# Attention and two MoE layers on one core: scratch in a later weight's place, eight early loads, and unread products on TensorE

## The chip, the cores and the metric

The kernel runs on one core of one Trainium2 chip. The metric is the device time of one execution in microseconds (us). TensorE is PE in the profile (its weight loads are PEld), VectorE is DVE, ScalarE is ACT, GpSimd is POOL, SyncE is SP. DMAs are asked for on SP, on ACT or on POOL; in the kernel before only SP and, late in the program, POOL ask for any. TensorE's clock has two levels, 1.2 and 2.4 GHz.

## The reference

Three layers, float32 (the weights of the first MoE come as 8-byte floats):

```python
# attention: q, k, v of (4, 8, 576, 64), s of (4, 8, 576)
cum = cumsum(maximum(s, 0), -1)
bias = -(cum[..., :, None] - cum[..., None, :])
scores = where(causal, -1e9, q @ k.T / sqrt(64) + minimum(bias, 0))
x = softmax(scores) @ v                      # reshaped to (2304, 512)
# first MoE layer: a dense gated block, 512 -> 2048 -> 512
h = x @ w_in
x = (h * sigmoid(1.702 * h)) @ w_out
# second MoE layer: 8 experts, every token in each of them, 512 -> 1024 -> 512
P = exp(logits - max); eight rounds of row and column normalisation, times N / E
out = sum over e of P[:, e] * (relu(x @ w1[e]) @ w2[e])
```

The running sums of `s` go into the scores as extra rows of the q and k operands.

## The kernel before, in words

The program is a list of instructions for each engine, and the order of each list is fixed when the kernel is built. A planner in the file (class `Sequencer`) sets it: it gives each instruction a cost and an earliest time, keeps a planned clock for each engine, and issues an engine's instructions in the order of their planned times. A loop near the end of the file (`while moe1_can is not None`) picks TensorE's next piece of work: the first of six kinds (scale of v, transposed x, values, transposed scores, scores, first MoE) that the plan holds ready. Where nothing is ready it moves TensorE's planned clock on, by at most 100 planned ns at a time, and looks again. So a wrong cost changes the order of the instructions, and nothing else.

Attention goes in groups of 8 heads: tokens 0 to 255 of a batch (one unit of work for each head), then tokens 256 to 575 (three units). A unit has scores (tile `sp`, on PE), a masked maximum (`sm`, `stats`, on DVE), an exponential (on ACT), a transpose (`tp`, on PE), a copy (`pf`, on ACT or DVE), the values (`op`, on PE), and a division into `xg` (DVE). The first eight heads take q and k as they come, in float32, from the tile `kf`: 64 rows by one DMA, and 2 rows of running sums by a second, from the small tile `aux0`, which DVE has to compute first (`sums(0, 256)`). There are four `kf` buffers (`N_KF`), so that heads 4 to 7 are loaded when earlier heads are done with theirs. Later heads load `kq`, split it into a rounded part and a rest (`one`, `two`) and fetch their rows of sums from DRAM (`aux_d`, written by `sums_left`, which the program comes to after the third unit of scores).

When 256 tokens are done they are transposed (`xtp`, `xh`, `xl`), and the first MoE can run on them: `mm1` makes 24 products into `hp`, and `mm2` 24 into `acc` (`accx`, `accw`), for each of 8 pairs of weight tiles. The weights come as chunks `st`, four to a pair, and ACT and DVE turn each into a rounded part and a rest (`wih`, `wil`, `woh`, `wol`). The memory holds four pairs (`NP0`) while the scratch of the early attention is allocated. The running sums (`aux0`, `aux`, `cum`) have a pool of their own, `auxpool`; when it is done, heads 8 to 15 take its place through `spool2`. The second MoE follows after the first and takes two thirds of the time; the change does not touch it.

Every DMA of the hardware queues reports on one of eight semaphores, in turn over all of them and whichever engine asks for it, and a DMA waits, on the engine that asks, until the last one on the same semaphore has landed. In the rows of the built program they stand as DMAHW0 to DMAHW7.

Of the kernel before, what the change touches and what calls it, by code (L numbers as in the profile page):

```python
# [38 lines left out]
N_KF = 4  # L39
# [18 lines left out]
class Sequencer:  # L58
# [96 lines left out]
    def submit(self, engine, what, call, outs, ins, adds=False):  # L155
        op = Op()
# [4 lines left out]
        if what == "dma_start":  # L161
            op.cost = 60 if engine == "SP" else 1000
            op.nbytes = self.size(outs[0]) * outs[0].shape[0] * (2 if self.fine and outs[0].dtype == F16 else 4)
            if adds and self.fine:
                op.nbytes *= ADDING
        else:
            sums = len(outs) > 1
            if engine == "PE":
                op.load = 110 if BYTES[ins[0].dtype] == 4 else 27
            op.cost = self.cost(engine, what, outs[0], ins, sums)  # L170
            op.tail = {"DVE": 85, "ACT": 110}.get(engine, 0) + 90 * sums
# [31 lines left out]
    def issue(self, op):  # L203
# [9 lines left out]
        if op.nbytes:  # L213
            self.issued = max(self.issued, start) + 475
            self.dma = max(self.dma, self.issued + 1200) + op.nbytes / 360
            op.end = self.dma + 440 + op.late
# [119 lines left out]
def kernel(  # L336
# [42 lines left out]
    NP0, NP1 = 4, 7  # L379
# [13 lines left out]
    alloc_w(wpool, range(NP0))  # L393
# [11 lines left out]
    su_aux = ExitStack()  # L405
    auxpool = Pool(seq, su_aux.enter_context(tc.tile_pool(name="auxpool", bufs=1, side=left, reuse_waits="tile")))
    aux0 = auxpool.tile([BH, 4, 256], F32, name="aux0")
    aux = auxpool.tile([2 * BH, 4, S], F32, name="aux")
    cum = auxpool.tile([2 * BH, 2, S], F32, name="cum")
# [37 lines left out]
    def sums_left():  # L447
# [4 lines left out]
        for t, p, r, by in ((1, slice(BH, 2 * BH), 0, 8.0), (0, slice(0, BH), 2, -1.0)):  # L452
# [6 lines left out]
            nc.sync.dma_start(out=aux_d[:, :, t], in_=aux[p])  # L459

# [115 lines left out]
    spool2 = []  # L576

    def place_of(n):
        if n < H:
            return spool  # L580
        if n >= 2 * H:
            return apool
        if not spool2:
            su_aux.close()
            spool2.append(Pool(seq, su.enter_context(
                tc.tile_pool(name="spool2", bufs=1, side=left, reuse_waits="tile")
            ), aux.tensor.name))
        return spool2[0]

# [12 lines left out]
    def load_qk(n):  # L602
# [3 lines left out]
        if n < H:  # L606
            kq = spool.tile([66, kend + nq], F32, tag="kq", name="kf", bufs=N_KF)
            nc.sync.dma_start(out=split_qk(kq[0:64], q0), in_=of_qk(qk[b, h, 0:64], n))
            nc.sync.dma_start(out=kq[64:66], in_=aux0[b * H + h:b * H + h + 1])
            qk_of[n] = (kq,)  # L610
            return
        kq = place_of(n).tile([128, kend + nq], F32, tag="kq", name="kq", bufs=3 if n < 2 * H else 1)
# [20 lines left out]
    def load_more():  # L633
        nonlocal n_qk
        while n_qk < min(len(heads), n_scored + 1 + N_KF if n_qk < H else n_prep + (3 if n_qk < 2 * H else 1)):
            if n_qk == H and (n_s < 3 or auxpool.held()):
                return
# [311 lines left out]
    def do_score():  # L949
# [13 lines left out]
        if n_s == 3:  # L963
            sums_left()
# [185 lines left out]
    def convert():  # L1150
# [12 lines left out]
        if c == 4 * NP0 and stage[0] is spool:  # L1163
            if n_s < NU and units[n_s][0] < 2 * H - 2 or n_v < NU and units[n_v][0] < 2 * H - 2:
                return
            if min(n_pv, n_prep) < 2 * H or spool.held() or spool2[0].held():
                return
# [8 lines left out]
        if c == 4 * NP1 and NP1 not in wih:  # L1176
# [5 lines left out]
            )), range(NP1, NPAIR))  # L1182
        seq.rank = 2
# [669 lines left out]
    seq.holding = True  # L1853
    sums(0, 256)
    for n_qk in range(1, 3):
        load_qk(n_qk - 1)
# [53 lines left out]
    def first_moe():  # L1910
# [3 lines left out]
        def can(j):  # L1914
            p = at_pair[j]
            if p == NPAIR or 4 * p + 2 > n_conv:
# [3 lines left out]
                seq.settled(wih[p].tensor.name), seq.settled(wil[p].tensor.name),  # L1920
            )

        def second(i):
            def when():
# [3 lines left out]
                t = max(seq.settled(x.tensor.name) for x in (gh, gl, woh[p], wol[p]))  # L1928
# [9 lines left out]
        for item in range((NB1 - 2) * NPAIR):  # L1938
# [6 lines left out]
            if (j, p) == (1, 0):  # L1945
                lent[0] = True
            mm1(j, p, 0)
# [62 lines left out]
    while moe1_can is not None:  # L2010
# [14 lines left out]
        if which is None:  # L2025
            stuck += 1
            assert stuck < 3000
            seq.free["PE"] = min(min(times), now + 100)
# [252 lines left out]
```

## Time and profile before

| | us |
|---|---|
| median of 3 runs (2004.87 to 2005.23) | 2005.07 |
| the profiled execution, whole | 2004.55 |
| its span, from the first instruction to the last | 2002.8 |
| PE busy in the span (15683 products) | 1963.7 |
| DVE busy | 1472.6 |
| ACT busy | 1252.9 |

The profiled execution is 0.5 us below the median, and 1.75 us of it lie outside its span. The rows come from one execution: start and length of instructions, what they waited for, the busy time of each engine in a stretch, and PEclk, the granted TensorE clock as a share of 2.4 GHz. The ends of matmuls are modelled, so the distance from one start to the next says more of the speed of TensorE than the length does.

### The profile page before, as it was taken

Reading aid. Unit: us, or ns where it says so; the run is one execution under the profiler, and the core shown is the slowest. Engines: PE = TensorE matmul, PEld = TensorE weight load, DVE = VectorE, ACT = ScalarE, POOL = GpSimd, SP = SyncE. Lnnn points to the kernel's source line nnn. Section 1 sums busy time; section 2 is a strip of 40 time slices with the busy share of each in tenths; the row PEclk is TensorE's granted clock in tenths of the full one; section 3 lists DMA queues with packets and bytes.
Section 4 is the critical chain, followed back from the end, with each engine's and each line's share of the span. In section 5 each row is a group of like instructions: output and inputs, shape, how many; then the busy total and the mean of one; then the engine's idle time right before and its main releaser. Section 6 shows DMA issues by size and latency. Waiting matters only on the chain.

```text
span 2002.8 us, 40907 instructions
## 1 busy us (share of the span) xinstructions
PE 1963.7 (98%) x15683; PEld 1581.9 (79%) x15683; DVE 1472.6 (74%) x3416; ACT 1252.9 (63%) x2581; POOL 87.5 (4%) x144
## 2 busy tenths in 40 slices
PE   7999999999999999999999999999999999999999
PEld 6889999999988677777777777777777777777777
DVE  5887799887753676988877766776786876777656
ACT  5887677666644575666666666656666666665333
POOL 0000000000000000000000111111101001111000
PEclk9989999999999999999999999999999999999999
DMA  7455345444226454475475566767557556666331
GB/s 222 157 187 172 115 141 171 133 119 123 75 69 213 156 197 151 158 257 182 156 256 144 132 183 176 182 170 204 161 129 245 151 150 185 165 171 182 119 129 43
DMA packets 230100, 322.11 MB, mean 161 GB/s; under 512 B 38272, under 2 KB 156224, under 8 KB 229904
## 3 DMA queue, kind: packets, MB, share of 16 engines
q1 hardware_dynamic: 216944, 295.90, 45.2%
q0 software_dynamic: 12960, 23.60, 8.3%
q8 instruction: 123, 2.02, 0.4%
q14 instruction: 73, 0.60, 0.1%
HBM read 230.85 MB, written 84.34 MB: 157 GB/s over the span
## 4 chain that ended last, share of the span: by engine, by line
PE 81%; DVE 9%; ACT 6%; DMA 3%; issue 1%; SPq 0%; POOL 0%; ACTq 0%; DVEq 0%; POOLq 0%
PE C L294 16%; PE A L294 16%; PE D L294 16%; PE hp L294 8%; PE B L294 8%; PE acc L294 5%; PE sp L294 3%; PE op L294 3%; PE tp L294 2%; ACT h L294 2%; PE accw L294 2%; DVE h L294 2%; DVE hst L294 1%; DMA kq<-in_qk_dram 1%; PE accx L294 1%
## 5 line engine op out<-in xcount | busy, mean ns | idle before, releaser
L294 PEld LDWEIGHTS <-h 128*128 128x128 f16 x6048 | 591.4, 98 | 85.6 <-issue 6.9
L294 PEld LDWEIGHTS <-w1o 128*128 128x128 f16 x4036 | 394.6, 98 | 255.1 <-issue 4.4
L294 PE MATMUL C<-xt,w1o 128*128 128x384 f16 x1152 | 218.6, 326 | 1.4 <-DVE hst L294 1.4
L294 PE MATMUL D<-xt,w1o 128*128 128x384 f16 x1152 | 218.4, 326 | 0.0
L294 PE MATMUL D<-w2o,h 128*128 128x256 f16 x1728 | 217.7, 273 | 0.2 <-ACT y L294 0.2
L294 PE MATMUL A<-xt,w1o 128*128 128x384 f16 x1152 | 214.8, 326 | 0.1
L294 PE MATMUL A<-w2o,h 128*128 128x256 f16 x1728 | 212.2, 273 | 1.8 <-ACT B L294 1.6
L294 PE MATMUL C<-w2o,h 128*128 128x256 f16 x1728 | 208.4, 273 | 1.8 <-DVE y L294 1.7
L294 DVE SCALAR_TENSOR_TENSOR h<-hst,h 128x768 f16<-128x768 f32 (+1 forms) x192 | 138.7, 751 | 56.0 <-ACT h L294 56.0
L294 ACT COPY C<-B 128x384 f32<-128x384 f32 (+1 forms) x168 | 71.5, 426 | 153.6 <-PE B L294 92.6
L294 PE MATMUL hp<-xh,wih 128*128 128x256 f32 (+1 forms) x512 | 156.3, 305 | 0.5 <-DVE t L294 0.5
L294 PE MATMUL hp<-xl,wih 128*128 128x256 f32 (+1 forms) x512 | 154.0, 301 | 0.0
L294 PE MATMUL hp<-xh,wil 128*128 128x256 f32 (+1 forms) x512 | 153.3, 299 | 0.0
L294 POOL DMA_DIRECT2D acc_d<-y x90 | 78.0, 867 | 1219.6 <-DVE y L294 660.3
L294 ACT ACTIVATE h<-hst 128x768 f16<-128x768 f32 (+1 forms) x192 | 126.2, 678 | 3.8 <-DVE hst L294 3.7
L294 ACT ACTIVATE sm<-sm,stats 64x576 f32<-64x576 f32 (+4 forms) x160 | 93.0, 601 | 41.6 <-DVE stats L294 41.2
L294 PE MATMUL acc<-gh,woh 128*128 128x256 f32 x384 | 111.1, 289 | 0.0
L294 PE MATMUL B<-w2o,h 128*128 128x256 f16 x864 | 110.5, 273 | 0.1
L294 PE MATMUL B<-xt,w1o 128*128 128x384 f16 x576 | 109.3, 326 | 0.0
L294 PE MATMUL acc<-gl,woh 128*128 128x256 f32 x384 | 108.5, 282 | 0.0
L294 PE MATMUL acc<-gh,wol 128*128 128x256 f32 x384 | 108.3, 282 | 0.0
L294 ACT COPY B<-A 128x384 f32<-128x384 f32 (+1 forms) x168 | 70.3, 426 | 57.9 <-PE A L294 57.2
(235 smaller groups left out, 3880.3 us busy)
## 6 DMA issues: line engine op xcount, KB each, us to landing
xt<-xc_d SPq DMA_DIRECT2D x168, 384.0 KB
wm<-in_moe_w_dram SPq DMA_DIRECT2D x112, 256.0 KB
w2o<-w_d SPq DMA_DIRECT2D x56, 512.0 KB
wr<-in_moe_w_dram SPq DMA_DIRECT2D x112, 256.0 KB
w_d<-wo SPq DMA_DIRECT2D x98, 256.0 KB
acc_d<-y POOLq DMA_DIRECT2D x90, 256.0 KB, 5.0
kq<-in_qk_dram SPq DMA_DIRECT2D x32, 448.0 KB
st<-in_moe_w_in_dram SPq DMA_DIRECT2D x16, 512.0 KB
```

The lines of the kernel that those rows point to most:

```text
L294: self.seq.submit(self.name, what, lambda: method(*args, **named), outs, ins, "accum_op" in named)
```

## The change

- The running sums get no pool of their own. They lie in `auxw`, a tile in the place where the fifth pair of weights goes later, so `NP0` is 5. `sums_left` is called at the start, right behind `sums(0, 256)`.
- `kf` of the first eight heads lies in two buffers each of the first MoE's tiles `gh`, `gl`, `t` and two of its own. All eight are asked for at the start; six of the eight loads, and the rows of sums of every second head, are asked for on ACT. Heads 8 to 15 have two `kq` buffers (three before).
- TensorE gets products of a constant bf16 tile `filler` into `unread`, which nothing reads: 14 of 512 columns at the start, and one of 128 columns at every second look of the loop that finds nothing ready for over 100 planned ns, until the first MoE's first piece.
- The planner holds TensorE at its high level from the end of the 14 on, counts a DMA on SP as 450 planned ns in place of 60 up to the second MoE, one on ACT as 600, and looks at parts of tiles where it looked at whole ones.

```diff
-N_KF = 4
+N_FILL = 14
-            op.cost = 60 if engine == "SP" else 1000
+            op.cost = 1000 if engine == "POOL" else 600 if engine == "ACT" else 60 if self.fine else 450
-            self.issued = max(self.issued, start) + 475
+            self.issued = max(self.issued, start) + 475 if self.fine else start + op.cost
-    NP0, NP1 = 4, 7
+    NP0, NP1 = 5, 7
-    alloc_w(wpool, range(NP0))
+    alloc_w(wpool, range(NP0 - 1))
+    auxw = wpool.tile([128, 32 * 128], F32, tag="last", name="auxw")
-    aux0 = auxpool.tile([BH, 4, 256], F32, name="aux0")
-    aux = auxpool.tile([2 * BH, 4, S], F32, name="aux")
-    cum = auxpool.tile([2 * BH, 2, S], F32, name="cum")
+    aux0 = auxw[2 * BH:3 * BH, 0:1024].rearrange("p (r s) -> p r s", r=4)
+    aux = auxw[0:2 * BH, 0:4 * S].rearrange("p (r s) -> p r s", r=4)
+    cum = auxw[0:2 * BH, 4 * S:6 * S].rearrange("p (t s) -> p t s", t=2)
+    filler = spool.tile([128, 512], BF16, name="filler")
+    nc.vector.memset(filler, 1.0)
+    unread = ps_m.tile([128, 512], F32, tag="acc0", name="unread")
+    def fill(n):
+        nc.tensor.matmul(unread[:, 0:n], lhsT=filler[:, 0:128], rhs=filler[:, 0:n], start=True, stop=True)
-            kq = spool.tile([66, kend + nq], F32, tag="kq", name="kf", bufs=N_KF)
-            nc.sync.dma_start(out=split_qk(kq[0:64], q0), in_=of_qk(qk[b, h, 0:64], n))
-            nc.sync.dma_start(out=kq[64:66], in_=aux0[b * H + h:b * H + h + 1])
+            tag = ("gh", "gl", "t", "kf")[n // 2]
+            kq = (spool if tag == "kf" else mpool).tile([128, kend + nq], F32, tag=tag, name="kf", bufs=2)[0:66]
+            ask = nc.scalar if n > 1 else nc.sync
+            ask.dma_start(out=split_qk(kq[0:64], q0), in_=of_qk(qk[b, h, 0:64], n))
+            ask = nc.scalar if n % 2 else nc.sync
+            ask.dma_start(out=kq[64:66], in_=aux0[b * H + h:b * H + h + 1])
-        kq = place_of(n).tile([128, kend + nq], F32, tag="kq", name="kq", bufs=3 if n < 2 * H else 1)
+        if n < 2 * H:
+            kq = spool.tile([128, kend + nq], F32, tag="kq", name="kq", bufs=2)
+        else:
+            kq = apool.tile([128, kend + nq], F32, tag="kq", name="kq", bufs=1)
-        if n_s == 3:
-            sums_left()
+    for _ in range(N_FILL):
+        fill(512)
+    seq.cold = False
     sums(0, 256)
+    sums_left()
...
-            seq.free["PE"] = min(min(times), now + 100)
+            if filling[0] and stuck % 2 and min(times) > now + 100:
+                fill(128)
+            else:
+                seq.free["PE"] = min(min(times), now + 100)
```

The list of ACT at the program's start, before, with buffer numbers (the rows `sm` are the exponentials of the units, `pf` is a copy):

```order
L294 ACT_TABLE_LOAD
L294 COPY stats_124<-stats_124 128x1
L294 ACTIVATE sm_231<-sm_231,stats_124 128x128
L294 ACTIVATE sm_231<-sm_231,stats_124 128x256
L294 ACTIVATE sm_244<-sm_244,stats_124 128x128
L294 ACTIVATE sm_244<-sm_244,stats_124 128x256
L294 ACTIVATE sm_265<-sm_265,stats_124 128x128
L294 COPY pf_280<-tp_276 128x384
```

and the same place now (`kf_221` to `kf_228` are heads 0 to 7) and with the semaphores that each row waits for:

```order
L294 COPY stats_119<-stats_119 128x1 [waits Pool_49]
L294 DMA kf_223<-in_qk_dram 64x2x256 [waits DMAHW1_49]
L294 DMA kf_224<-in_qk_dram 64x2x256 [waits DMAHW3_49]
L294 DMA kf_225<-in_qk_dram 64x2x256 [waits DMAHW4_49]
L294 DMA kf_226<-in_qk_dram 64x2x256 [waits DMAHW5_49]
L294 DMA kf_227<-in_qk_dram 64x2x256 [waits DMAHW6_49]
L294 DMA kf_228<-in_qk_dram 64x2x256 [waits DMAHW7_49]
L294 DMA kf_222<-auxw_88 2x1x512 [waits DMAHW1_49,DVE_49]
L294 DMA kf_224<-auxw_88 2x1x512 [waits DMAHW2_49]
L294 DMA kf_226<-auxw_88 2x1x512 [waits DMAHW3_49]
L294 DMA kf_228<-auxw_88 2x1x512 [waits DMAHW4_49]
L294 ACTIVATE sm_268<-sm_268,stats_119 128x128 [waits DVE_49]
```

Ten DMAs have come to stand ahead of ACT's first exponential, the rows of sums of head 1 behind the loads of heads 2 to 7.

The list of SP at the start, now (the rows from the third DMA on; `vf` are values, `aux_d` the sums in DRAM):

```order
L294 DMA vf_131<-in_v_dram 128x8x64
L294 DMA vf_132<-in_v_dram 128x8x64
L294 DMA kf<-auxw 2x1x512 [waits DVE_49,Pool_49]
L294 DMA kf<-auxw 2x1x512 x2
L294 DMA kf<-auxw 2x1x512 [waits DMAHW0_49]
L294 DMA aux_d<-auxw 128x1x576 [waits DMAHW2_49,DVE_49,Pool_49]
L294 DMA aux_d<-auxw 128x1x576 [waits DMAHW0_49,DVE_49]
L294 DMA st<-in_moe_w_in_dram 128x2x512 [waits DMAHW5_49]
```

SP asks for the sums of heads 0, 2, 4 and 6, on semaphores 5, 6, 7 and 0; before, it asked for those of heads 0 to 3 here, and for `aux_d` only after those of heads 4 to 7.

The list of PE at the end of the 14 long products, as a piece of the difference (`unread` is the new product, `sp` with `kf` the scores of the first heads, two rows to a head):

```order
+L294 MATMUL unread<-filler 128x512
+L294 LDWEIGHTS filler
+L294 MATMUL unread<-filler 128x128
+L294 LDWEIGHTS filler
+L294 MATMUL unread<-filler 128x128
 L294 MATMUL sp<-kf 128x128
 L294 MATMUL sp<-kf 128x256
 L294 MATMUL sp<-kf 128x128
 L294 MATMUL sp<-kf 128x256
+L294 LDWEIGHTS filler
+L294 MATMUL unread<-filler 128x128
```

Before, the list begins with the scores of heads 0, 1 and 2 and the first transposes. Now two short products stand ahead of the scores of heads 0 and 1, and two behind them; then, as before, come the scores of head 2 and the first transposes. Up to the first `hp` there are 59 short products: 4 at these two places, 15 in runs of 8 and 7 before the last values of the first eight heads, and 40 in runs of 5, 3, 2, 16 and 14 between those values and the transposes of heads 8 and 9. The run of 16 stands right behind the eight `xtp`, and the run of 14 behind the `vbp` that follows it. The first `hp` now come in two runs of 12 with scores, values and transposes around them; before, the first was one run of 24.

## Rows read from the trace of the kernel before

**Rows 1.** Windows: stretch, length, busy time (instructions) of each engine, PEclk, DMA share, GB/s
```profile
12.64:35.80 23.16, 22.44 (x93) 20.03 (x91) 13.98 (x56) 15.01 (x32) 0.14 (x1) 1.00 0.88 264
35.80:43.92 8.12, 4.51 (x15) 3.54 (x16) 7.97 (x24) 5.21 (x9) 0.00 (x0) 1.00 0.54 152
43.92:48.00 4.08, 4.08 (x19) 3.74 (x18) 3.99 (x10) 2.95 (x5) 0.00 (x0) 1.00 0.66 228
...
48.00:100.00 52.00, 47.89 (x386) 41.87 (x384) 43.41 (x134) 44.30 (x79) 0.88 (x6) 0.99 0.52 162
...
120.00:180.00 60.00, 55.29 (x473) 53.42 (x471) 52.94 (x138) 50.61 (x104) 0.29 (x2) 0.89 0.61 190
180.00:582.00 402.00, 397.25 (x3874) 379.70 (x3873) 323.10 (x972) 267.14 (x552) 3.20 (x22) 1.00 0.45 128
```

**Rows 2.** Timeline of PE, 46 to 49 us: start, length, instruction, [idle before <-releaser]
```profile
45.92 0.41 PE L294 MATMUL hp<-xh,wil 128*128 128x256 f32 x1
46.14 0.41 PE L294 MATMUL hp<-xh,wih 128*128 128x256 f32 x1
...
48.16 0.28 PE L294 MATMUL hp<-xl,wih 128*128 128x256 f32 x1
48.28 0.28 PE L294 MATMUL hp<-xh,wil 128*128 128x256 f32 x1
```

**Rows 3.** Timeline of PE, 99 to 170 us: the waits ahead of low stretches
```profile
99.66 0.60 PE L294 MATMUL vbp<-vd,ones_b 8*128 8x16 f32 x2 [2.03 <-DVE vd L294]
...
118.41 0.36 PE L294 MATMUL sp<-two 68*128 68x256 f32 x1 [2.46 <-DMA two<-one]
...
123.28 0.88 PE L294 MATMUL tp<-ident,sm 128*128 128x128 f32 x3 [2.25 <-DVE stats L294]
...
169.93 0.45 PE L294 MATMUL sp<-one 128*128 128x384 f32 x1 [1.66 <-DVE stats L294]
```

**Rows 4.** Windows over the three stretches in which the granted clock is low
```profile
99.20:106.02 6.82, 6.36 (x46) 6.06 (x47) 5.99 (x18) 2.44 (x5) 0.17 (x1) 0.50 0.15 42
119.69:126.51 6.82, 4.57 (x30) 4.38 (x28) 6.09 (x22) 5.54 (x15) 0.00 (x0) 0.50 0.26 71
170.88:177.71 6.83, 6.35 (x37) 5.80 (x38) 4.96 (x11) 5.05 (x10) 0.14 (x1) 0.50 0.35 106
```

**Rows 5.** Timeline of DVE, 10 to 18 us: first maximum, and the second half's sums
```profile
10.45 0.29 DVE L294 CUSTOM_DVE_ANT_0 sm<-sp,mask 128x128 f32<-128x128 f32 x1 [4.86 <-PE sp L294]
...
12.16 0.31 DVE L294 TENSOR_SCALAR cum<-cum 64x320 f32<-64x320 f32 x1
...
16.20 1.53 DVE L294 SCALAR_TENSOR_TENSOR aux<-cum,aux 32x576 fp32r<-32x576 f32 x2
```

**Rows 6.** Timeline of SP's queue (SPq), 1 to 21 us
```profile
1.50 1.25 SPq L294 DMA_DIRECT2D kf<-in_qk_dram  x2
...
5.73 2.62 SPq L294 DMA_DIRECT2D kf<-aux  x4
...
20.44 0.89 SPq L294 DMA_DIRECT2D st<-in_moe_w_out_dram  x1
```

**Rows 7.** Chain of waits, first 50 us: start, length, what
```profile
5.73 2.80 DMA kf<-aux
```

**Rows 8.** Timeline of ACT, 10 to 23 us
```profile
10.78 0.85 ACT L294 ACTIVATE sm<-sm,stats 128x128 f32<-128x128 f32 x2 [7.66 <-DVE stats L294]
...
22.42 0.67 ACT L294 ACTIVATE st<-st 128x512 f32<-128x512 f32 x1 [1.03 <-DMA st<-in_moe_w_out_dram]
```

**Rows 9.** Timeline of PE, 12 to 15 us
```profile
12.64 0.85 PE L294 MATMUL tp<-ident,sm 128*128 128x128 f32 x3
13.28 1.49 PE L294 MATMUL sp<-kf 66*128 66x128 f32 x4
14.56 0.85 PE L294 MATMUL tp<-ident,sm 128*128 128x128 f32 x3
```

**Rows 10.** Page, costliest groups: count, busy us, mean ns of one, idle before
```profile
L294 PEld LDWEIGHTS <-h 128*128 128x128 f16 x6048 | 591.4, 98 | 85.6 <-issue 6.9
```

## What I predicted before the run

> **What bounds the kernel now.** I read three views in this order. First the busy time by stretches, to see where TensorE (PE) is not full. From 180 to 582 us it is busy for 397.25 of 402 us [rows 1], and nothing that the change does can win more than the 4.75 us there. Before 180 us it is not: of the 60 us from 120 on it misses 4.7, of the 52 us from 48 on 4.1, of the 8.12 us from 35.80 on 3.6 [rows 1]. In these stretches VectorE (DVE) is busy for 52.94 of 60, 43.41 of 52 and 7.97 of 8.12 us: where PE waits there, DVE is mostly what it waits for.
>
> Second, PE's timeline, for its speed. At 46 us two neighbouring products of 256 columns start 0.22 us apart, at 48.2 us 0.12 apart [rows 2]. 256 columns in 0.213 us is 1.2 GHz. So PE runs at its low level until about 48 us, although PEclk reads 1.00 there. The scores of the first heads say the same from the start: one head has 128 and 256 columns in four float32 passes, 1536 columns, and its four records take the 1.28 us from 13.28 to 14.56, which is again 1.2 GHz [rows 9]. From 12.64 to 35.80 us PE is busy for 22.44 of 23.16 us, with DVE at 13.98 and ScalarE (ACT) at 15.01 [rows 1]. So the first eight heads are bound by a slow PE, and 23 us of busy PE did not lift the level: it rose in the first run of 24 dense `hp`. At the high level those 22.44 us would be 11.2.
>
> Here the Trainium skill bears on the reading: "TensorE: Matmul & The Clock Gate", section "Seeing it yourself", says that the recorded clock events were seen to be unreliable on trn2 and should be checked against the durations. By the record alone (1.00), the low start would not exist, and holding the level would be worth nothing; this trace has 0.22 against 0.12 us, so the durations decide.
>
> Third, the waits. PE falls to 0.50 at 99.20, 119.69 and 170.88 us and stays there for 6.82 us each time [rows 4]; ahead of each fall it had idled for 2.03, 2.46 and 1.66 us in one piece, the last with further short waits behind it, and a wait of 2.25 us lies inside the second low stretch [rows 3]. That is the measure for the new idle time below: a gap of some 2 us is enough to lose the level.
>
> **The change part by part.** The sum is made against the profiled execution (2004.55, span 2002.8) and put on the median of 2005.07, which is 0.5 higher.
>
> *Start of the scores.* The 14 long products need only a constant, so they can start as soon as DVE has written it, some 1.4 us into the span by the engines' first rows (SP's first loads stand at 1.5 [rows 6]). At the low level 512 columns are 0.427 us (twice 0.213), 14 of them 6.0 us, and they end near 7.4. They are as dense as the `hp` that lifted the level, so I expect the high level by their end. Now what follows them. The sums of head 0 are asked for on SP 0.31 us later than before, since the second half's maximum stands ahead of the scan on DVE [rows 5]: 5.73 + 0.31 = 6.04, and they land 2.80 us later [rows 7], at 8.84. Head 0's scores then take 0.64 us at the high level and end at 9.48. Head 1's sums stand on ACT, behind the loads of heads 5, 6 and 7, and these wait on the semaphores 5, 6 and 7 that SP's sums of heads 0, 2 and 4 hold. At 0.65 us for an issue (four of SP's took 2.62 [rows 6]): head 5's load goes at 8.84, head 6's at 9.49, head 7's at 10.14, head 1's sums at 10.79, and they land 2.80 later, at 13.59. PE idles from 9.48 to 13.59, 4.1 us. The other end: issues on ACT that cost nothing, and landings after 1.98 us (a 512 KB chunk went from its issue at 20.44 to its reader at 22.42 [rows 6, 8]): 6.04 + 1.30 + 1.98 = 9.32, and 11.30 for head 1; the gap is then 11.30 less (8.02 + 0.64), 2.6 us. Both ends are over 2.03 us, so the level is lost again before head 1, and the first eight heads run at 1.2 GHz as they did.
>
> Then the first transposes wait for head 1 (1.28), two short products (0.2) and head 2 (1.28): 13.59 + 2.76 = 16.35, against 12.64 before [rows 9]; at the other end 14.06. That is +3.7 or +1.4; I take +3.0, nearer to the end whose durations are of the same DMA. Queued behind ACT's ten DMAs is the first exponential: 10.79 + 4 x 0.65 = 13.4 in place of 10.78 [rows 8]. The transposes wait for it, but PE is at head 2 until 16.35, so it costs nothing more. SP's next rows, `aux_d`, wait for DVE's sums; weight chunks stand behind them and are not needed for 30 us.
>
> The skill weighs this otherwise: "DMA: Bandwidth & Descriptors", section "Issuing engines are not separate DMA queues", says that a second issuing engine only saves the sequencer's time to initiate a DMA, which is usually small beside the DMA. By that alone the start would cost 0.31 and no more, and the sum below would be 2.7 lower (2007.4). No row of before shows a DMA on ACT; what it waits for is read from the new list of instructions.
>
> *Short products.* 55 of the 59 lie between head 1's scores and the first `hp`. At the low level 128 columns take 0.107 us, half of 0.213; with a load of 128 columns (98 ns in the page [rows 10]) that nothing hides, 0.2. That is 5.9 or 11 us. At the other end they are free, where PE would have waited: before, it idled for 0.72 us up to 35.80 and for 3.61 up to 43.92 [rows 1]. But 8 score rows of the next heads now stand in the same place (about 2.5 us at the low level), and the plan counted PE twice as fast as it will run, so that PE gets to most of these products late. I take 5.9 less 1.4 hidden, +4.5 (ends 0 and +11).
>
> *When the level rises.* Before, at 48 us, inside the first 24 `hp`. Now the runs of 16 and 14 may lift it a little earlier, or the broken `hp` (12 and 12) may not lift it until the next run of 24. The PE work from the second run of short products to the first `hp` is some 5 us, from there to the run of 24 about 8 at the high level: -4 to +8. I take 0.
>
> *The other sums.* The second half's sums (six rows from the one of 0.31 us to the pair of 1.53, 3.7 us together [rows 5]) move from between the scores into the 4.86 us in which DVE idles ahead of its first maximum [rows 5]. Between the scores PE was the bound, so the gain is nothing (0 to -3.7). Without that cover, head 0's first maximum would start at their end, and PE is waiting for head 1 in any case.
>
> *Fifth pair, two `kq` buffers, dearer SP in the plan.* They reorder everything after the first `hp`. At stake is what is lost between 80 and 182 us: the waits of rows 3 and half of the busy time at the low level, (6.36 + 4.57 + 6.35) / 2 = 8.6 us [rows 4]. The wait of 2.46 us for `two<-one` is one that a plan with dear SP issues should see coming: -2.5. A buffer less could add another like it (+2.5), and the ends for the whole reorder are -17 (all waits of rows 3, 8.4, and the 8.6) and +10 (two more falls of 3.2 us each with their gaps of 2).
>
> Sum: +3.0 + 4.5 + 0 - 2.5 = +5.0, so 2010.1 us.
>
> **The rivals.**
> 1. *The level holds through the first eight heads; faster.* Place: head 1's scores. It decides at a gap of about 2 us: if her sums land within that of head 0's end, PE never idles as long as it did ahead of the three falls. Price: 22.44 us of PE become 11.2, but DVE has 13.98 us to do there, and at the share it reaches later (43.41 of 52, 0.83 [rows 1]) that is 16.8, so the 23.16 us shrink by 6.3; the 4.08 us from 43.92 on halve (-2.0); the short products fall into true gaps (0); +0.5 at the start; -2.5 later: -10.3, 1995. For it: the products at the start are dense and early. Against it: both ends of the gap (2.6, 4.1) are over it.
> 2. *The later order gives back more than the start loses.* The first two falls of rows 4 and their waits vanish: -(6.36 + 4.57) / 2 - 2.03 - 2.46 - 2.25 = -12.2; with +7.5 from the first two terms, -4.7: 2000.4. For it: the planned cost of an SP issue comes from 60 to near what rows 6 show (0.4 to 0.9 us). Against: the stretch of plain attention before the next `xtp` stays, and DVE's share there with it.
> 3. *The lag is hidden.* From 48 to 120 us DVE is busy for 0.83 of the time and PE waits for it; if DVE makes up in its idle 17% what PE lost, the end is where it was: 2005, give or take 4. Against: after 180 us PE has hardly a gap, so what is lost before is lost.
> 4. *The level stays low up to the unbroken 24 `hp`.* +8 on top: 2018.
> 5. *The record is right and the level was high all along.* Then the short products cost 55 x 0.055 = 3.0 us and the start +3: near 2009. The distances of rows 2 speak against it.
>
> **How the numbers follow.** My forecast 0.33, rival 1 0.12, rival 2 0.14, rival 3 0.26, rival 4 0.13, rival 5 0.02. What this measurement can tell from no change is about 0.2%, 4.0 us: faster is under 2001.1, slower over 2009.1. Faster: rival 1 whole, rival 2 in two cases of three (0.09), and some 0.03 each of rival 3 and of my forecast: 0.27. Slower: rival 4 whole, three quarters of my forecast (0.25), rival 5 and a few hundredths of the others: 0.44. The rest, 0.29, is within. The range may leave out two in ten: from 1994, which takes rival 1's time in, to 2019, over rival 4's. My forecast's own range is 2003 to 2016.
>
> **What would show it.** In the profile of the changed kernel: the long products end near 7.4 us; PE idles 2.6 to 4.1 us between head 0's and head 1's scores; four records of one head take 1.28 us again (0.64 would be rival 1); ACT's first exponential stands between 11.5 and 13.5 us; the last values of head 7 end at 39 to 42 us (35.8 before), the first `hp` starts at 53 to 57 (43.92 before), where rival 1 has it before 40. Busy PE from 48 to 180 us tells rivals 2 and 3 apart. I am wrong if head 1's sums land before 11 us, if a gap of 2.6 us keeps the level, or if the first `hp` comes before 50 us.

## The result, and the profile after

The changed kernel takes 2020.82 us (median of 4 runs, 2018.56 to 2024.75) against 2004.97; the ratio is 1.0081, 95% interval 1.0063 to 1.0100. It is slower, by 12.6 to 20.0 us. I had said slower, at 2010.1, with 2019 as the upper end: the time lies 1.8 us over the range, and 10.7 over the forecast. The profiled execution took 2018.97, span 2017.3.

Where the two profiled executions stand apart, read from PE's timelines (a piece is a run of 24 `hp`, the first half of one item of the first MoE):

| start of | before | after | apart by | by my sum |
|---|---|---|---|---|
| the first transposes | 12.64 | 18.20 | +5.6 | +3.0 |
| the first `hp` | 43.92 | 55.89 | +12.0 | +7.5 |
| the 5th piece | 124.81 | 124.42 | -0.4 | |
| the 57th piece | 576.94 | 579.96 | +3.0 | +5.0 |
| the 63rd piece | 640.35 | 654.97 | +14.6 | +5.0 |
| end of the span | 2002.8 | 2017.3 | +14.5 | +5.0 |

So 12.0 us were lost up to the first `hp`, 12.4 came back up to the 5th piece, 3.4 were lost again up to the 57th, and 11.6 in a place that the prediction does not mention.

The timeline of PE in the changed kernel (start, length, instruction, idle before and what ended it), which answers to [rows 9]:

```profile
1.53 6.25 PE L294 MATMUL unread<-filler 128*128 128x512 bf16 x16 [1.53 <-DVE filler L294]
8.41 0.89 PE L294 MATMUL sp<-kf 66*128 66x128 f32 x4 [0.63 <-DMA kf<-in_qk_dram]
15.16 1.65 PE L294 MATMUL sp<-kf 66*128 66x128 f32 x4 [5.86 <-DMA kf<-auxw]
...
18.20 0.85 PE L294 MATMUL tp<-ident,sm 128*128 128x128 f32 x3
18.84 1.49 PE L294 MATMUL sp<-kf 66*128 66x128 f32 x4
20.12 0.85 PE L294 MATMUL tp<-ident,sm 128*128 128x128 f32 x3
```

Head 0's scores are fast, then PE waits 5.86 us for head 1's sums. From 18.84 to 20.12 a head takes 1.28 us again. ACT's timeline shows what head 1's sums stood behind (ACTq is its DMA queue); SP's sums of heads 0, 2, 4 and 6 were asked for from 6.47 on, 0.74 us later than before [rows 6]:

```profile
4.46 6.92 ACTq L294 DMA_DIRECT2D kf<-in_qk_dram  x6
11.48 3.14 ACTq L294 DMA_DIRECT2D kf<-auxw  x4
14.67 0.80 ACT L294 ACTIVATE sm<-sm,stats 128x128 f32<-128x128 f32 x2 [11.42 <-DMA kf<-in_qk_dram]
```

Busy time by stretches (length, PE, PEld, DVE, ACT, POOL, then PEclk, DMA share, GB/s), after:

```profile
10.00:15.00 5.00, 0.00 (x0) 0.00 (x0) 0.48 (x4) 0.33 (x2) 0.00 (x0) 0.59 0.83 243
15.00:45.00 30.00, 29.27 (x128) 25.89 (x129) 12.58 (x60) 16.10 (x35) 0.14 (x1) 0.50 0.55 171
45.00:50.00 5.00, 4.79 (x38) 4.25 (x37) 4.97 (x18) 4.44 (x8) 0.00 (x0) 0.65 0.24 79
...
175.00:190.00 15.00, 11.62 (x91) 9.81 (x91) 10.92 (x26) 10.67 (x22) 0.14 (x1) 0.77 0.58 183
...
55.89:124.40 68.51, 63.63 (x546) 56.24 (x545) 59.07 (x180) 59.00 (x112) 1.01 (x7) 0.95 0.58 181
```

and the last stretch's counterpart before:

```profile
43.92:124.80 80.88, 71.81 (x595) 64.26 (x594) 67.66 (x207) 64.26 (x122) 1.04 (x7) 0.93 0.49 154
```

The level is low from 10.9 to 48.5 us. From the first `hp` to the 5th piece the stretch is 12.4 us shorter. PE idles for 4.9 us in place of 9.1 (4.2). The mean clock goes from 0.93 to 0.95, which at half speed is 5.7 less 3.4 us (2.3). To this come 2.0 us that the 0.93 leaves out: before, the 4.08 us from 43.92 to 48.00 ran at the low level under a PEclk of 1.00 [rows 1, 2]. The rest, some 4 us, is PE work that no longer stands in the stretch (546 products, 595 before): some 34 products of the attention now come ahead of the first `hp`, and some 16 behind the 5th piece. So the 12.0 us up to the first `hp` are not all loss, and the 12.4 are not all gain. From 175 to 190 us a wait of 2.48 us for a maximum and a low stretch behind it stand in the place of the third fall of [rows 3, 4], some 11 us later; the low stretch is as long as before (6.8 us).

The tail: the last two blocks of tokens go through the first MoE together, in wide steps (products of 512 columns, two steps to a pair of weights). PE's longest wait from 560 us on, and ACT's timeline there, after:

```profile
PE accw L294 <- DVE gh L294: 8.8, 1, 8.8
```

```profile
614.40 0.62 ACT L294 CAST gh<-t 128x512 fp32r<-128x512 f32 x1 [0.75 <-DVE t L294]
626.48 0.63 ACT L294 ACTIVATE wm<-wm 128x512 f32<-128x512 f32 x1 [11.46 <-DMA wm<-in_moe_w_dram]
...
630.75 0.58 ACT L294 ACTIVATE t<-hp 128x512 f32<-128x512 f32 x1
```

DVE's and PE's there, after:

```profile
632.15 0.43 DVE L294 CAST gh<-t 128x512 fp32r<-128x512 f32 x1
632.63 0.79 PE L294 MATMUL accw<-gh,wlast 128*128 128x512 f32 x1 [8.80 <-DVE gh L294]
```

and ACT's timeline before:

```profile
621.57 0.60 ACT L294 ACTIVATE t<-hp 128x512 f32<-128x512 f32 x1 [3.47 <-PE hp L294]
622.92 0.62 ACT L294 CAST gh<-t 128x512 fp32r<-128x512 f32 x1 [0.76 <-DVE t L294]
623.45 0.63 ACT L294 ACTIVATE wm<-wm 128x512 f32<-128x512 f32 x1
```

`wm` are pieces of the second MoE's weights, of which ACT takes squares. They are asked for on SP behind 7 loads `xt` and 14 `w1o`, from 617.75 us on before and from 620.95 on after, 3 us apart as everything there is. Before, ACT first made two more `gh` and then found the first piece landed. After, it came to the squares behind the `gh` of 614.40 and stood there for 11.46 us. Behind the first squares stood the activation `t` of 630.75, from which DVE made the `gh` of 632.15 that PE waited 8.8 us for; PEclk is 0.50 from 628.7 to 639.0 us. The cause is one line (experiment 1 tests it): `first_moe` calls `begin_weights` at the wide step `(p, i) == (NP0 - 1, 0)`, and `p` counts down, so `NP0 = 5` calls it two steps earlier.

### The profile page after: what moved, and what is told of

It reads as the page before. It is cut to its first block, busy times and chain, and to the rows that moved or that the text cites. A ratio compares the mean times of both kernels' runs of the same rounds, so it can differ in the third digit from the quotient of the medians.

```text
span 2017.3 us, 41015 instructions
## 1 busy us (share of the span) xinstructions
PE 1975.0 (98%) x15756; PEld 1585.4 (79%) x15756; DVE 1473.6 (73%) x3418; ACT 1252.1 (62%) x2580; POOL 87.3 (4%) x144
## 4 chain that ended last, share of the span: by engine, by line
PE 79%; DVE 9%; ACT 6%; DMA 4%; issue 1%; SPq 0%; ACTq 0%; DVEq 0%
PE C L294 16%; PE A L294 16%; PE D L294 16%; PE B L294 8%; PE hp L294 7%; PE acc L294 5%; PE op L294 3%; PE sp L294 3%; PE tp L294 2%; ACT h L294 2%; PE accw L294 2%; DVE h L294 2%; DMA kq<-in_qk_dram 1%; DVE hst L294 1%; PE accx L294 1%
## 5 line engine op out<-in xcount | busy, mean ns | idle before, releaser
L294 PE MATMUL hp<-xh,wih 128*128 128x256 f32 (+1 forms) x448 | 136.3, 304 | 0.0
L294 PE MATMUL hp<-xl,wih 128*128 128x256 f32 (+1 forms) x448 | 134.1, 299 | 0.0
L294 PE MATMUL hp<-xh,wil 128*128 128x256 f32 (+1 forms) x448 | 133.8, 299 | 0.0
L294 DVE SCALAR_TENSOR_TENSOR t<-t,hp 128x512 f32<-128x512 f32 x72 | 49.2, 683 | 72.4 <-ACT t L294 72.0
L294 ACT ACTIVATE h<-sb 128x768 f16<-128x768 f32 x96 | 80.8, 842 | 26.9 <-DVE sb L294 26.1
L294 PE MATMUL acc<-gh,woh 128*128 128x256 f32 x336 | 97.2, 289 | 0.0
```

Source lines behind the costliest of these rows:

```text
L294: self.seq.submit(self.name, what, lambda: method(*args, **named), outs, ins, "accum_op" in named)
```

## Experiments

All ratios are to the kernel before, run beside each; "after" is the changed kernel (1.0081).

**1. The tail.** Begin at the old step:

```diff
-            if (p, i) == (NP0 - 1, 0):
+            if (p, i) == (NP0 - 2, 0):
```

> The first loads of the second MoE's weights, and ACT's squares of the weight pieces (wm) behind them, are begun at the pair before last of the wide steps, two wide steps later than in the changed kernel and where the kernel before had them. Theory 1 (the squares stand too early on ACT and hold up the cast that PE's accw waits for): the one wait of 8.8 us of accw for gh near 626 us and the low level behind it (10 us at 0.55) go, worth 11 to 12 us, so 2007 to 2010. Rival (the step from hp 56 to hp 62 is slow for another cause, and the squares only fill a hole): the gap stays near 9 us and the time stays at 2018 to 2025. All else, the first 600 us above all, as in the changed kernel under both.

2009.67 us (11 runs, 2006.12 to 2013.19), ratio 1.0022 [1.0013, 1.0030]: theory 1. The wait for `gh` is gone, and ACT's timeline is in the old order again:

```profile
628.40 0.62 ACT L294 CAST gh<-t 128x512 fp32r<-128x512 f32 x1 [0.75 <-DVE t L294]
629.26 0.63 ACT L294 ACTIVATE wm<-wm 128x512 f32<-128x512 f32 x1 [0.24 <-DMA wm<-in_moe_w_dram]
```

The second run leaves the loads `xt` and `w1o` where they are, and moves the squares two wide steps later, with the `wm` loads that feed them:

```diff
         seq.rank = 0
-        second_expert()
...
+            if (p, i) == (NP0 - 2, 0):
+                second_expert()
```

> The loads of the second MoE's weights stay at the earlier place; only ACT's squares of the wm pieces, with their loads, are asked for two wide steps later. Theory 1a (the squares' place in ACT's order alone makes the wait): as the run with both later, 2007 to 2010, and no wait of accw for gh over 2 us. Rival 1b (the early loads, or the memory given up early, make the wait): 2018 to 2025 as in the changed kernel.

2010.93 us (8 runs), ratio 1.0025 [1.0015, 1.0035], no such wait: theory 1a, 0.9 us over its range. On SP the `wm` loads still come right behind the `w1o` (from 627.26 us on, the last `w1o` done at 626.85). So the squares' place on ACT made the loss, not the early `xt` and `w1o` or the memory.

**2. The start.** All rows of sums on SP, the loads left on ACT:

```diff
-            ask = nc.scalar if n % 2 else nc.sync
-            ask.dma_start(out=kq[64:66], ...
+            nc.sync.dma_start(out=kq[64:66], ...
```

> All eight rows of sums of the first heads are asked for on SP; the six loads stay on ACT. Theory 2 (head 1's sums come late because they stand on ACT behind loads that wait for SP's sums): the idle 5.9 us between head 0's and head 1's scores shrinks below 1.5 us, and the first transpose comes at 13 to 15 us (18.20 in the changed kernel). With it the level may hold through the first eight heads (then the first hp comes at 35 to 45 us, 55.89 in the changed kernel); if a gap of 1 us or DVE's waits lose it, at 48 to 53. On the time: theory 3 (the stretch from the first hp to 120 us is bound by DVE and hides the lag of the start): unchanged, within 3 us of the changed kernel's 2020.8; rival (a lag at the start is kept to the end): 5 to 12 us less, 2009 to 2016.

2008.64 us (9 runs, 2006.17 to 2014.17), ratio 1.0020 [1.0010, 1.0030]. PE's timeline:

```profile
1.53 4.67 PE L294 MATMUL unread<-filler 128*128 128x512 bf16 x16 [1.53 <-DVE filler L294]
9.17 1.55 PE L294 MATMUL sp<-kf 66*128 66x128 f32 x8 [2.97 <-DMA kf<-auxw]
10.56 0.28 PE L294 MATMUL unread<-filler 128*128 128x128 bf16 x2
10.93 1.46 PE L294 MATMUL sp<-kf 66*128 66x128 f32 x4
12.62 1.00 PE L294 MATMUL tp<-ident,sm 128*128 128x128 f32 x3 [0.23 <-ACT sm L294]
```

Head 1 follows head 0 with no gap, and the first transposes come at 12.62, sooner than I had expected and as before the change: theory 2. The first `hp` comes at 50.0, and the whole is 12.2 us faster than after, a little more than the rival had (2009 to 2016): this speaks against theory 3. The edit also moves the plan's order behind the start, which experiment 4 holds still. The level falls all the same, during head 2. The tail's wait (8.7) is still there.

**3. Both mended.**

> The two edits that helped, together: second MoE's first loads and squares two wide steps later, and all rows of sums of the first heads asked for on SP. If the two losses are separate (tail 11.2 us by 2020.8 less 2009.7; start and its reorder 12.2 us by 2020.8 less 2008.6), their sum: 2020.8 - 23.4 = 1997, that is 8 us under the kernel before. Rival (the run with the sums on SP alone had won part of the tail already, as its profiled 2014 beside a median of 2008.6 leaves open): 2003 to 2009.

1999.10 us (12 runs, 1994.25 to 2003.42), ratio 0.9969 [0.9959, 0.9979]. The losses are separate within the noise: the tail's edit is worth 11.8 us alone and 10.2 with the other, the start's 12.2 and 10.6 (differences of the ratios by 2005). Mended, the change is 6.2 us faster than the kernel before.

**4. Is a late start hidden?** The kernel before with 36 extra maxima on DVE ahead of the sums, every engine's list otherwise in the same order:

```diff
+    for _ in range(36):
+        x = cum[:, 0, 0:256]
+        tc.nc.vector.tensor_scalar(out=x, in0=x, scalar1=0.0, scalar2=None, op0=ALU.max)
     seq.holding = True
     sums(0, 256)
```

> The kernel before, in its own order, with 36 extra maxima on DVE ahead of the running sums, so that everything in the first eight heads starts some 10 to 13 us later (first transpose at 23 to 26 us in place of 12.64, first hp at 52 to 57 in place of 43.92). Theory 3 (the stretch from the first hp to 120 us waits for DVE and takes up a late start whatever the order): 2003 to 2009, as before. Rival (a late start is kept, and the changed kernel's order alone made up for it): 2014 to 2018.

2016.24 us (5 runs), ratio 1.0056 [1.0044, 1.0068], or +11.2 us. PE's timeline:

```profile
19.86 4.18 PE L294 MATMUL sp<-kf 66*128 66x128 f32 x12 [19.86 <-DMA kf<-aux]
23.83 0.85 PE L294 MATMUL tp<-ident,sm 128*128 128x128 f32 x3
```

The first transposes are 11.2 us late, and the end is 11.2 us late. DVE is late here as well as PE, as in the changed kernel, where it waits 6.37 us for head 1's scores. Theory 3 fell: the stretch that waits for DVE gives nothing back when its work is the same. What stood level at the 5th piece in the changed kernel was a loss of 12.0 and a better order.

**5. What holds the level.** With both mended, 24 long products in place of 14, to fill the gap ahead of head 0:

```diff
-N_FILL = 14
+N_FILL = 24
```

> As the run with both mended, with 24 long products in place of 14, so that TensorE has no idle time of over 1 us ahead of head 0's scores (2.97 us in the run with the sums on SP). Theory 5 (the level fell near 10.5 us there because of the 2.97 us idle ahead of head 0): the level holds, four records of a head take 0.64 us for heads 2 to 7 too, the last values of head 7 end near 28 us (36.6 there) and the first hp comes at 38 to 46 us (50.0). Rival 5b (float32 scores, transposes and values of the first heads do not hold the level, however dense): heads 2 to 7 take 1.28 us and the first hp stays at 49 to 52. On the whole time: if DVE hides what PE wins up to 120 us, within 3 us of the run with both mended; if not, up to 8 us less.

2005.50 us (12 runs, 2000.25 to 2013.74), ratio 1.0004 [0.9992, 1.0017]. PE's timeline, and its windows:

```profile
1.54 7.09 PE L294 MATMUL unread<-filler 128*128 128x512 bf16 x24 [1.54 <-DVE filler L294]
8.80 1.55 PE L294 MATMUL sp<-kf 66*128 66x128 f32 x8 [0.17 <-DMA kf<-auxw]
...
10.56 0.92 PE L294 MATMUL sp<-kf 66*128 66x128 f32 x4
...
12.24 1.49 PE L294 MATMUL sp<-kf 66*128 66x128 f32 x4
```

```profile
8.00:12.00 4.00, 3.70 (x19) 2.27 (x18) 3.48 (x14) 1.04 (x4) 0.00 (x0) 0.99 0.44 126
12.00:16.00 4.00, 4.00 (x17) 3.53 (x16) 1.02 (x7) 2.69 (x8) 0.00 (x0) 0.50 0.75 207
```

0.17 us of idle time ahead of head 0, and the level is gone at 12 us, with PE busy for 4.00 of the next 4.00 us. Theory 5 fell; 5b holds from head 3 on: the gap ahead of head 0 did not decide. Then the same with one bf16 product behind each piece of work up to head 7's last values:

```diff
             (do_vpow, do_flush, do_value, do_turn, do_score)[which]()
+            if filling[0] and n_v < H:
+                fill(512)
```

> As the run with 24 long products, with one more unread bf16 product of 512 columns behind each piece of TensorE's work (scores, transpose, values) up to the last values of head 7. Theory 6 (the level falls behind head 2, with PE busy, because the float32 scores, transposes and values do not hold it; bf16 products among them would): four records of a head take 0.64 us for all eight heads, three transposes 0.32 (0.64 at the low level), and head 7's last values end at 26 to 33 us. Rival (the short idle times between the pieces decide, or so few bf16 products are too little): 1.28 us a head as in the run with 24 alone, the added products take 0.43 us each at the low level and head 7's values end at 42 to 48 us. On the whole time: the start says little (theory 3), so 1995 to 2009 under both.

2002.30 us (12 runs, 1998.70 to 2014.35), ratio 0.9998 [0.9984, 1.0011]. Windows:

```profile
12.00:16.00 4.00, 3.34 (x17) 2.21 (x18) 1.05 (x7) 1.78 (x5) 0.00 (x0) 1.00 0.88 253
16.00:20.31 4.31, 0.00 (x0) 0.03 (x1) 0.57 (x4) 1.55 (x4) 0.00 (x0) 0.77 0.97 312
20.31:24.70 4.39, 4.39 (x18) 3.95 (x19) 2.05 (x6) 3.88 (x10) 0.00 (x0) 0.50 1.11 276
24.70:28.00 3.30, 3.30 (x22) 2.83 (x21) 2.25 (x13) 2.32 (x5) 0.00 (x0) 0.93 0.89 330
```

Now the level holds from 12 to 16 us though PE is busy for less (3.34 of 4.00, with a wait of 0.73). It falls in a wait of 4.31 us for a copy that stands on ACT behind work on a weight chunk that had not landed, and comes back near 24.7 us, among the mixed work. Theory 6 holds for the level; head 7's last values start only at 37.7, not by 33, and the time is 1.2 us under that of the 24 alone, which the noise covers.

**6. The products.** Mended, with none of them; and the changed kernel with the long ones alone:

```diff
-N_FILL = 14
+N_FILL = 0
...
-            if filling[0] and stuck % 2 and min(times) > now + 100:
+            if False:
```

> As the run with both mended, with no unread products at all (the 14 long and the short ones are left out). If the products are worth nothing because the first eight heads run at 1.2 GHz either way and the stretch to 120 us hides the start: within 3 us of the run with both mended. Rival (the long ones save 0.64 us on each of heads 0 and 1, the runs of short ones lift the level at 41 us rather than inside the first hp, and that is kept): 4 to 8 us more.

2004.35 us (12 runs), ratio 0.9992 [0.9983, 1.0000]: 4.6 us over the run with both mended. The products win, for the rival.

> No short products (55 of 128 columns up to the first hp are left out; the 14 long ones stay). Theory 4 (they only stand in the way of the scores): the first hp comes 3 to 5 us sooner (51 to 53 us), the level rises in the first hp as in the kernel before, and the time is unchanged within 3 us, since the stretch to 120 us hides it. Rival 4b (the two runs of 16 and 14 ahead of the first hp lift the level at 48 us): without them the first 24 hp run at 0.22 us apart, hp 2 comes no sooner than 83 us, and the time is 2018 to 2027. The wait of 8.8 us near 626 us stays under both.

2016.02 us (5 runs), ratio 1.0055 [1.0043, 1.0067], 5 us faster than after, though the intervals touch. The first `hp` came at 56.6, not sooner. The level was high from 47.2 to 50.6 us, where PE mostly waited (busy for 0.61 of 3.40), and then from 54.0 on; in the changed kernel it was high from 48.5 on. So 4b was right that the short products lift the level for good sooner, by 5.5 us, but its sign did not come: the first `hp` stand 0.12 us apart. The time fell out of both ranges. In this order the short products seem to cost; whether it is they or the plan's order around them is not shown. And the kernel before with the products alone (the 14, the short ones, and the plan's high level, put in as in the change):

> The kernel before with the unread products alone (14 long ones at the start, short ones in the plan's gaps up to the first MoE, and the plan at the high level from the start). Theory 8 (the products are what made the order with both mended faster than before: 5.2 of its 6.4 us): 1998 to 2003. Rival (they only win together with the other parts, and here stand in the way of the scores, as my term of +4.5 said): 2004 to 2012.

2006.33 us (12 runs), ratio 0.9999 [0.9991, 1.0008]: neither theory 8 nor my +4.5. The profiled execution was 6.6 us ahead at the 5th piece (118.2) and 1.4 behind at the 57th (578.4). What the products are worth differs between the three kernels; that the plan's order around them decides it is likely, and not shown.

**7. The planner.** Both mended, with a DMA on SP at 60 planned ns again:

```diff
-            op.cost = 1000 if engine == "POOL" else 600 if engine == "ACT" else 60 if self.fine else 450
+            op.cost = 1000 if engine == "POOL" else 600 if engine == "ACT" else 60
```

(and the planned time of the next DMA as before).

> As the run with both mended, but the planner counts a DMA on SP as 60 planned ns again. If the dearer SP is what made the later order better (my term of -2.5 us, and the rival in which the later order gives back 12): 2 to 12 us more than the run with both mended, with a wait of some 2 us for two<-one and a low stretch near 120 us again. If the order after the first hp moves with anything (each order draws its own low stretches): within 4 us either way.

2001.07 us (10 runs), ratio 0.9983 [0.9973, 0.9992], 2.8 us over the run with both mended, and the intervals touch: inconclusive, near my -2.5. PE's waits for `two<-one` were no longer (2.2 us in all from 40 to 200 us, against 3.6).

**8. Other orders, and the level held.** 13 and 17 long products, then each with the mixture of part 5:

> As the run with both mended (14 long products, 1999.1), with 13. Nothing that lasts is changed, 0.2 to 0.4 us at the start; the planner gives TensorE and DVE another order after the first heads. If each order draws its own waits and low stretches up to 120 us (theory 7): a time anywhere from 1995 to 2008, with the difference to 1999.1 there at the fifth group of hp. Rival (the time follows the start, which is the same): 1998 to 2000.

> As the run with both mended, with 17 long products. Theory 7 (each order draws its own waits and low stretches): a time anywhere from 1995 to 2008. Rival (the time follows the start): 1998 to 2000; or (the long products themselves cost, as 24 were 6.4 us slower than 14): 2000 to 2002, between the two.

1996.62 us (5 runs), ratio 0.9962 [0.9950, 0.9974], and 1997.31 (5 runs), 0.9965 [0.9953, 0.9977]. Neither can be told from the run with 14 (0.9969), so theory 7 is not shown by these; only the 24 stand apart.

> As the run with both mended and 13 long products (1996.6), with one more bf16 product of 512 columns behind each piece of TensorE's work up to head 7's last values. Theory 9 (a level held among the float32 work is worth what my first rival said, some 6 us up to the first hp, and is kept as a late start was): 1988 to 1994. Rival (what the first heads win, DVE or ACT gives back before 300 us): 1995 to 2003. Under both the four records of a head take 0.64 us for most heads where no idle time of over 3 us lies before.

> As the run with both mended and 17 long products (1997.3), with the same mixture. Theory 9: 1988 to 1994. Rival: 1995 to 2003.

1995.62 us (6 runs), ratio 0.9942 [0.9929, 0.9955], and 1990.79 (6 runs, 1987.13 to 1995.45), 0.9923 [0.9911, 0.9936]. Beside 13 and 17 without the mixture that is 4.0 us (the intervals touch) and 8.4 us (beside 24 it was 1.2): theory 9's range for 17, the rival's for 13. With 17, windows:

```profile
16.00:20.00 4.00, 3.41 (x24) 2.56 (x23) 0.71 (x5) 1.67 (x4) 0.00 (x0) 1.00 1.16 277
20.00:25.00 5.00, 3.14 (x19) 2.15 (x19) 4.44 (x19) 4.02 (x9) 0.00 (x0) 1.00 1.00 337
25.00:35.00 10.00, 9.34 (x36) 7.48 (x37) 4.56 (x20) 5.39 (x12) 0.00 (x0) 0.51 0.90 294
```

The level holds to 25 us, with seven heads at 0.66 to 0.73 us, falls in a wait of 1.28 us for ACT (I had named 3 us), and is back at 35.4. With 13 the level fell already at 10.2, but was back at 13.7 and held to 92 us; a window of that stretch, and one of the low stretch with 13 and no mixture:

```profile
13.70:45.00 31.30, 27.01 (x203) 21.57 (x202) 22.96 (x90) 24.53 (x49) 0.29 (x2) 1.00 0.79 244
10.30:41.00 30.70, 30.12 (x134) 26.21 (x132) 15.01 (x75) 17.17 (x36) 0.15 (x1) 0.50 0.70 219
```

So the level was held best with 13, and the time moved most with 17. And theory 9's "some 6 us up to the first hp" did not come: in the profiled executions the first `hp` starts 1.2 us (13), 1.8 (17) and 2.4 (24) sooner than without the mixture, and with 17 and 24 head 7's last values end later (38.5 against 36.9, and 38.6 against 36.1). An estimate of why: the mixture adds 29, 25 and 23 products of 512 columns, which at 0.21 us from start to start are 6.2, 5.3 and 4.9 us of PE. Where the 8.4 us with 17 come from is not shown; the two profiled executions are 2.8 us apart. This kernel is the fastest here, 15.4 us under the one before.

## Why the prediction was right and wrong

**The step that failed** is "*Fifth pair, two `kq` buffers, dearer SP in the plan.* They reorder everything after the first `hp`. At stake is what is lost between 80 and 182 us", with -2.5 and ends of -17 and +10. Up to the 57th piece it came to -9.0 (-12.4, then +3.4). But the step ends at 182 us and puts everything behind it at nothing: `NP0` also sets when the second MoE's weights are begun, and that costs 10 to 12 us at 615 to 640 us (experiment 1). The text ahead of the prediction even says that the change does not touch the second MoE. In the profiled executions the parts are +12.0 up to the first `hp` (my sum: +7.5), -9.0 from there to the 57th piece (-2.5) and +11.6 behind it (0). Without the last the kernel is at 2009.67, 0.4 us from my number; that agreement is luck, since the other two were off by 4.5 and 6.5 us in opposite directions.

**Start of the scores, +3.0 (1.4 to 3.7).** The mechanism was right: ACT's loads wait for landings of SP's DMAs, and head 1's sums stand behind them. The size was not: the gap was 5.86 us, not 2.6 to 4.1. ACT was done with its six loads at 11.38, where I had 10.79, and head 1's scores began 3.68 us after her sums were asked for, where I had 2.80 from one landing. The size also differs between executions: with the same DMAs at the start, head 1's scores begin at 15.16 us in the changed kernel, at 17.30 and 15.43 in the two runs of experiment 1, and at 16.06 in the one without short products. The edit that takes this wait away is worth 10.6 to 12.2 us by the medians (experiments 2, 3), and the first `hp` starts 5.9 and 8.8 us sooner with it; where the rest is won is not shown (the profiled execution of experiment 2, 2014.17, is the slowest of its nine). I had taken from the Trainium skill ("DMA: Bandwidth & Descriptors", section "Issuing engines are not separate DMA queues") that by its sentence alone the start would cost 0.31. The sentence speaks of the time to initiate a DMA; what cost here was that the second issuing engine waited for the first one's DMAs, and the first transposes came 5.6 us later.

**Short products, +4.5 (0 to +11).** Inside its range and wrong as a term: 5 us lost in the changed kernel (the intervals touch), 4.6 won with both mended (all products), nothing in the kernel before (all products).

**When the level rises, 0 (-4 to +8).** Right: at 48.5 us, as before (48.0), now in the short products ahead of the first `hp`.

**The measure "a gap of some 2 us is enough to lose the level"** was wrong as used. I put the fall down to idle time and had rival 1 decided by head 1's gap. In experiment 5 the level fell without a gap, in dense float32 work, and held over short gaps with bf16 products in between. In the changed kernel itself it fell at 82.6 us with no wait over 0.28 us in the 8 us before. And in the kernel before with the products alone PE waited 2.66 us up to 670.6 us, and the level stayed high (1.00 from 668 to 680 us). The page of before had shown it: 22.44 of 23.16 us busy and never high. I had written that and still laid the blame on the gap.

**The rivals.** Rival 1 (the level holds, -10.3) did not happen in the change, and its price was not borne out: with the level held over most of the first heads by added products, the first `hp` came 1.2 to 2.4 us sooner, not 6.3, and the time went down by 1.2, 4.0 and 8.4 us, of which only the last is clear of the noise. Rival 2 (the later order gives back 12.2) did happen in size, 12.4 between the first `hp` and the 5th piece, though only 8.5 of it are waits and low clock; the rest is work moved ahead or behind. Rival 3 (the lag is hidden) looks right at the 5th piece; experiment 4 disproves it for an unchanged order. Rival 4 did not occur, rival 5 is excluded: heads take some 0.7 or some 1.3 us. Going by the distances between products was right. The Trainium skill ("TensorE: Matmul & The Clock Gate", section "Seeing it yourself") warns that recorded clock events were seen to be unreliable on trn2, and asks for the throttled time to be set against the penalty of a cold clock; to look at durations in place of the record was my reading of it. No run here shows a wrong event: the first entry of the clock record in the trace of before is the rise at 48.0 us, and PEclk counts the time ahead of a first entry as 1.00. In the run without products that is so up to 56.0 us, with heads at 1.28.

**Signs.** Right: the long products' end (7.8), a head's 1.28 us, the first `hp` (55.89, in 53 to 57). Missed: PE's gap, ACT's first exponential (14.67, not 11.5 to 13.5), and head 7's last values by a little (42.8, not 39 to 42).

## What to carry over

A constant that names a place in memory may also set when a later stage starts: look up every use of it, and read the order of the in-order engines at each, however far from the edit. A wait for a DMA on an in-order engine costs what stands behind it, not what it does. And when a late start seems to vanish, delay it alone in the old order before calling it hidden.

## What the runs showed of the hardware

- Dense float32 work of the first heads did not keep TensorE's high level: 0.50 with PE busy for 4.00 of 4.00 us; with a bf16 product behind each piece it stayed at 1.00, with PE busy for 3.34 of 4.00.
- At a program's start PEclk reads 1.00 while the durations are those of 1.2 GHz, since the record has no entry yet (the first stands at 48.0 us before, at 7.5 after); behind the 14 long products record and durations agree (0.50 and 1.28 us from 15 to 45 us).
- Loads asked for on ACT wait, by the semaphores in the built program, for landings of SP's DMAs: six took 6.92 us to ask for (4.31 of issues and 2.61 of waiting between them), where four took SP 2.62 [rows 6].
- The runs of one kernel lie 4 to 16 us apart. With 24 long products the long ones have a lower mean clock (spans of 1997.9 at 0.992 and 2012.0 at 0.982); without products the clock does not tell them apart (1998.58 us at 0.996, 2007.16 at 0.997). Which of the short waits lose the level in which run stays open.
